# Attention, mixture of experts and MLP on one core: the first chunk's loads, splits and evacuations rearranged

## The chip, the cores and the metric

The kernel runs on one core of a Trainium2 chip. The metric is the device time of one execution in microseconds (us), the median of three runs. Before the change these were 749.26, 752.66 and 753.28 us, median 752.66.

## What is computed

Three stages follow each other, over two batches of 576 tokens.

```python
# attention: batch 2, heads 8, sequence 576, head size 64
scores = q @ k.T / 8
cum = cumsum(log(clip(f, 1e-4, 1)))                 # per head, along the sequence
scores = where(causal, -1e9, scores + cum[:, None] - cum[None, :])
attn = softmax(scores) @ v
x = attn as (1152 tokens, 512)
# mixture of 4 experts, 512 -> 1024 -> 512
p = domain_probs / (domain_probs.sum(-1) + 1e-9)
out = sum over e of p[:, e] * (relu(x @ w1[e]) @ w2[e])
# MLP, 512 -> 2048 -> 512
h = out @ w_in
y = (h * sigmoid(1.702 * h)) @ w_out
```

## The kernel before

**Tiles and stages.** The 1152 tokens form four chunks: chunk 0 is batch 0, tokens 0 to 255; chunk 1 the other 320 tokens of that batch; chunks 2 and 3 the same of batch 1. Attention of a chunk goes in units. A unit of chunk 0 is one head (eight units); a unit of the others is a head pair and 128 queries. Each unit passes scores on TensorE (L367), the row maximum on VectorE (L394), the exponential on ScalarE (L408), the sum's reciprocal on VectorE (L414, L415), the normalisation on GpSimd (`e`, L417), transposes on TensorE (`t`, L435), copies of them to SBUF (`ph`, L53), and per head pair the product with the values (`x`, L462). From it come `xh` (rounded, ScalarE L53) and `xl` (the rest, VectorE L471). Every expert or MLP product is made as three matmuls (hi by hi, hi by lo, lo by hi), so each weight tile is split into `whi` and `wlo` (`split_w`: `whi` on ScalarE L53 or GpSimd L50, `wlo` on VectorE L159).

**Order.** Attention and expert visits are interleaved by a pulling loop: while the experts' products of one chunk run, units of the next are pulled. While chunk 0 is pulled, the first expert half is multiplied head pair by head pair (`emit_first`, L551); the next visits use L530 and L574. Within an engine the instructions stand in the order that the tile scheduler chose by its own simulation of the timeline; each engine then works that list off in order.

**Loads.** Nearly all DMAs are issued by SP on one hardware queue: `fr` (gates), `kd`, `qd`, `vd` of head groups 0 to 3 and 4 to 7 of chunk 0, `wst` (two expert weight tiles, 512 KB, two buffers that come free when both `wlo` are made), `kq` and `vd` of a later head pair, and per head pair `cb` (two, 256 KB) and `cbs` (288 KB). The last two are the cumulated gates broadcast over partitions, from a copy `cumd` in DRAM; `cbs` has the two heads' rows on 64 partitions each (L332). `prep_cum` loads them three units ahead (LEAD) and GpSimd adds a triangular mask to them (L326, L329 for `cb`, L335 for `cbs`). `dpT` and `dpb` are the experts' probabilities, written to DRAM and read back broadcast.

**Chunk 0's mask term.** The key tile `kd` holds 64 rows of keys; row 64 is the cumulated gate, brought by a DMA from `cum` (L300); the query tile holds a constant in that row (L294). Rows 65 to 127 are zeroed by memsets (L292, L293), and the product runs over 128 rows.

Of the kernel before, what the change touches and what calls it, by code (L numbers as in the profile page):

```python
# [32 lines left out]
def attn_moe_mlp(ctx: ExitStack, tc: tile.TileContext, qk0, qk1, qk2, v0, vp, fg, dp, wa_moe, wb_moe, wa_mlp, wb_mlp, outT):  # L33
# [15 lines left out]
    def round_pool(out, in_):  # L49
        nc.gpsimd.tensor_scalar(out=out, in0=in_, scalar1=1.0, scalar2=1.0, op0=ALU.mult, op1=ALU.mult)  # L50

# [96 lines left out]
    def split_w(kind, v_, g):  # L148
        raw = raw_w.pop((kind, v_, g))
        p = wa_p if kind == "a" else wb_p  # L150
        hi = p.tile([128, 4, 128], F32R, tag="hi", name="whi")
        lo = p.tile([128, 4, 128], F32R, tag="lo", name="wlo")
        hf = hi.rearrange("p a c -> p (a c)")
        lf = lo.rearrange("p a c -> p (a c)")
        (round_pool if late or v_ <= 2 and g == 3 else round_act)(hf, raw)
        (wa if kind == "a" else wb)[v_, g] = (hi, lo)

        def rest():
            nc.vector.tensor_sub(lf, raw, f(hf))  # L159
            if visits[v_][0] < NMOE:  # L160
                if g % 2:
                    load_pair()
            else:
                w_split_n[0] += 1

        lo_due.append(rest)
# [118 lines left out]
    def load_plain(h0):  # L285
# [4 lines left out]
        for i, t in enumerate((kd, qd)):  # L290
            nc.sync.dma_start(out=t[0:64], in_=qk0[h0 // G, i].rearrange("d (g s) -> d g s", g=G))
        nc.gpsimd.memset(kd[64:128], 0.0)  # L292
        nc.gpsimd.memset(qd[64:128], 0.0)  # L293
        nc.gpsimd.memset(qd[64:65], 1.0 / NEG)  # L294
        groups[h0] = (qd, kd, vd)

    def load_plain_rest(h0):
        G, wk = 4, SA
        qd, kd, vd = groups[h0]
        nc.sync.dma_start(out=kd[64:65], in_=cum[h0:h0 + G, :wk])  # L300
        nc.sync.dma_start(out=vd, in_=v0[h0 // G].rearrange("p (t g d) -> p t g d", t=2, g=G))
        for g in range(G):
            heads[0, h0 + g] = dict(vd=vd[:, :, g, :], qd=qd[:, g], kd=kd[:, g])

# [115 lines left out]
    def emit_tr(c, u):  # L420
# [7 lines left out]
        for k, (q0, off, w, _) in enumerate(todo):  # L428
# [3 lines left out]
            for k0, k1 in [(0, min(nk, 4))] + [(4, 5)] * (nk > 4):  # L432
# [4 lines left out]
                for j, h in enumerate(hs if w == S else hs[k:k + 1] if len(hs) > 1 else hs):  # L437
                    r = 64 if w == S else 128
                    ph = ph_of[c, h]
                    ph = ph[:, 3:4, 0:64] if k0 else ph[:, 0:k1, o:o + r]  # L440
                    round_act(ph, cols[:, :, j * r:(j + 1) * r])

# [169 lines left out]
    nc.sync.dma_start(out=fr, in_=fg)  # L612
    nc.vector.memset(ones, 1.0)
    load_plain(0)
    nc.gpsimd.memset(mask, 0.0)
    nc.gpsimd.affine_select(out=mask[:, 128:], in_=mask[:, 128:], pattern=[[-1, 128]],
# [6 lines left out]
    for a, z in ((0, SA), (SA, S)):  # L623
# [3 lines left out]
                                     initial=cum[:, a - 1:a] if a else 0.0, op0=ALU.mult, op1=ALU.add)  # L627
    load_plain_rest(0)
    load_plain(4)
    load_plain_rest(4)  # L630
    nc.vector.tensor_scalar(out=fr, in0=cum, scalar1=1.0 / NEG, scalar2=None, op0=ALU.mult)
    nc.sync.dma_start(out=cumd, in_=fr)
    for _ in range(2):
        load_pair()
    round_pool(tri, mask[:, 128:])
    make_probabilities()
    load_heads(passes[1], 0)
    nc.sync.dma_start(out=dpb0, in_=dpT[0:1, :S].to_broadcast([128, S]))
    nc.sync.dma_start(out=dpb1, in_=dpT[1:2, :DPB1].to_broadcast([128, DPB1]))

# [15 lines left out]
    while ready[0] < 0:  # L656
        pull()
        if pulled[0] in (7, 8, 9, 10):
            split_w("a", 0, pulled[0] - 7)
            split_rest()  # L660
        while x_made[0] > x_used[0] and pulled[0] > 10:
            emit_first(x_used[0])
            x_used[0] += 1
# [95 lines left out]
```

## Time and profile before

| what | value |
|---|---|
| median of the three runs | 752.66 us |
| the profiled execution's own time | 752.34 us |
| its span, first to last instruction | 750.4 us |
| mean granted TensorE clock | 0.991 of full speed |
| busy: TensorE, VectorE, GpSimd, ScalarE | 724.2, 470.1, 307.5, 220.9 us |
| bytes moved by DMA | 67.24 MB |

TensorE is busy nearly all the time, so a stretch is worth reading only where TensorE stands still or runs at the lower clock. A wait in the profile is written as the waiting engine and line, an arrow, and what came last of the things it waited for.

### The profile page before, as it was taken

Reading aid. Unit: us, or ns where it says so; the run is one execution under the profiler, and the core shown is the slowest. Engines: PE = TensorE matmul, PEld = TensorE weight load, DVE = VectorE, ACT = ScalarE, POOL = GpSimd, SP = SyncE. Lnnn points to the kernel's source line nnn. Section 1 sums busy time; section 2 is a strip of 40 time slices with the busy share of each in tenths; the row PEclk is TensorE's granted clock in tenths of the full one; section 3 lists DMA queues with packets and bytes.
Section 4 is the critical chain, followed back from the end, with each engine's and each line's share of the span. In section 5 each row is a group of like instructions: output and inputs, shape, how many; then the busy total and the mean of one; then the engine's idle time right before and its main releaser. Section 6 shows DMA issues by size and latency. Waiting matters only on the chain.

```text
span 750.4 us, 11873 instructions
## 1 busy us (share of the span) xinstructions
PE 724.2 (97%) x4424; PEld 669.9 (89%) x4424; DVE 470.1 (63%) x1015; ACT 220.9 (29%) x551; POOL 307.5 (41%) x402
## 2 busy tenths in 40 slices
PE   3989989999999999889999999999999999999998
PEld 2556769787799999889999999999999999999998
DVE  5546555666665999999964334343999865424422
ACT  4665544565632101101111111112323232222220
POOL 6546425343232324563363334443464445324420
PEclk9899989999999999999999999999999999999999
DMA  8656543421225544635321011100222200000012
GB/s 247 197 180 168 173 143 113 138 84 61 84 57 191 165 119 139 200 112 169 115 83 57 29 29 57 56 1 2 64 60 80 79 0 1 1 1 1 1 43 85
DMA packets 29497, 67.24 MB, mean 90 GB/s; under 512 B 3032, under 2 KB 4576, under 8 KB 29440
## 3 DMA queue, kind: packets, MB, share of 16 engines
q1 hardware_dynamic: 29440, 66.48, 28.7%
q8 instruction: 35, 0.57, 0.3%
q14 instruction: 22, 0.18, 0.1%
HBM read 64.05 MB, written 2.41 MB: 89 GB/s over the span
## 4 chain that ended last, share of the span: by engine, by line
PE 73%; DVE 16%; DMA 4%; issue 3%; POOL 2%; ACT 1%; SPq 0%; POOLq 0%; DVEq 0%; ACTq 0%
PE m L574 32%; PE m L530 29%; PE s L367 5%; DVE wlo L159 4%; PE x L462 3%; PE t L435 3%; DVE wf L214 2%; DVE cvd L220 2%; DVE wf L222 2%; DVE tmp L588 1%; DMA wst<-in_wb_moe_dram 1%; DMA wst<-in_wa_moe_dram 1%; DVE xl L594 1%; DVE cvt L206 1%; DVE cvt L217 1%
## 5 line engine op out<-in xcount | busy, mean ns | idle before, releaser
L590 POOL TENSOR_TENSOR acc<-acc,tmp 128x384 f32<-128x384 f32 (+3 forms) x112 | 104.5, 944 | 146.9 <-DVE tmp L588 128.6
L574 PE MATMUL m<-hh,wlo 128*128 128x384 f32 (+2 forms) x640 | 129.0, 322 | 3.8 <-DVE wlo L159 3.8
L574 PE MATMUL m<-hh,whi 128*128 128x384 f32 (+2 forms) x640 | 130.6, 324 | 0.3 <-DVE tmp L588 0.3
L574 PE MATMUL m<-hl,whi 128*128 128x384 f32 (+2 forms) x640 | 129.5, 322 | 0.0
L530 PE MATMUL m<-xh,whi 128*128 128x384 f32 (+2 forms) x624 | 127.4, 324 | 0.5 <-POOL whi L50 0.3
L556 ACT ACTIVATE hh<-m 128x384 fp32r<-128x384 f32 (+2 forms) x112 | 49.5, 444 | 263.4 <-PE m L530 252.1
L530 PE MATMUL m<-xh,wlo 128*128 128x384 f32 (+2 forms) x624 | 125.1, 321 | 1.3 <-DVE wlo L159 1.3
L530 PE MATMUL m<-xl,whi 128*128 128x384 f32 (+2 forms) x624 | 125.8, 321 | 0.0
L159 DVE TENSOR_TENSOR wlo<-wst,whi 128x512 fp32r<-128x512 f32 x112 | 97.7, 874 | 27.2 <-ACT whi L53 15.1
L574 PEld LDWEIGHTS m<-hh,wlo 128*128 128x128 f32 x640 | 106.4, 190 | 8.0 <-DVE wlo L159 5.2
L574 PEld LDWEIGHTS m<-hh,whi 128*128 128x128 f32 x640 | 106.8, 190 | 5.4 <-issue 4.0
L574 PEld LDWEIGHTS m<-hl,whi 128*128 128x128 f32 x640 | 106.8, 190 | 3.5 <-issue 3.4
L530 PEld LDWEIGHTS m<-xh,whi 128*128 128x128 f32 x624 | 103.5, 188 | 4.7 <-issue 1.8
L530 PEld LDWEIGHTS m<-xh,wlo 128*128 128x128 f32 x624 | 103.5, 188 | 3.0 <-DVE wlo L159 1.8
L530 PEld LDWEIGHTS m<-xl,whi 128*128 128x128 f32 x624 | 103.6, 188 | 2.3 <-issue 2.0
L565 POOL TENSOR_TENSOR hl<-tmp,hh 128x384 fp32r<-128x384 f32 x48 | 53.6, 1116 | 90.4 <-ACT hh L53 90.4
L557 DVE SCALAR_TENSOR_TENSOR hl<-m,hh 128x384 fp32r<-128x384 f32 (+2 forms) x112 | 55.2, 493 | 52.8 <-ACT hh L556 52.8
L50 POOL TENSOR_SCALAR whi<-wst 128x512 fp32r<-128x512 f32 x62 | 46.5, 757 | 71.9 <-issue 26.8
L588 DVE TENSOR_TENSOR tmp<-m,dpb 128x384 f32<-128x384 f32 (+2 forms) x80 | 40.8, 512 | 41.7 <-PE m L574 35.1
L417 POOL TENSOR_SCALAR e<-e,sm 128x128 f32<-128x128 f32 (+4 forms) x72 | 43.9, 621 | 35.2 <-DVE sm L415 22.2
L563 DVE TENSOR_TENSOR tmp<-m,sg 128x384 f32<-128x384 f32 x48 | 26.6, 555 | 45.9 <-ACT sg L562 45.8
L408 ACT ACTIVATE e<-e,mx 128x128 f32<-128x128 f32 (+4 forms) x72 | 41.9, 582 | 29.6 <-DVE mx L394 28.0
(74 smaller groups left out, 719.1 us busy)
## 6 DMA issues: line engine op xcount, KB each, us to landing
wst<-in_wa_moe_dram SPq DMA_DIRECT2D x28, 512.0 KB, 4.1
wst<-in_wb_moe_dram SPq DMA_DIRECT2D x28, 512.0 KB, 3.7
mst<-in_wa_mlp_dram SPq DMA_DIRECT2D x16, 512.0 KB, 3.9
mst<-in_wb_mlp_dram SPq DMA_DIRECT2D x16, 512.0 KB, 4.1
cb<-cumd SPq DMA_DIRECT2D x16, 256.0 KB, 5.7
vd<-in_vp_dram SPq DMA_DIRECT2D x8, 320.0 KB, 7.5
kq<-in_qk_dram SPq DMA_DIRECT2D x4, 608.0 KB, 6.5
cbs<-cumd SPq DMA_DIRECT2D x8, 288.0 KB
```

The source lines that it names most:

```text
L50: nc.gpsimd.tensor_scalar(out=out, in0=in_, scalar1=1.0, scalar2=1.0, op0=ALU.mult, op1=ALU.mult)
L159: nc.vector.tensor_sub(lf, raw, f(hf))
L367: nc.tensor.matmul(pt[:, :z - a], lhsT=l, rhs=r, start=True, stop=True)
L408: nc.scalar.activation(out=e[:, off:off + w], in_=e[:, off:off + w], func=AF.Exp, scale=-1.0, bias=mx, accum_out=sm[:, 0, k:k + 1])
L417: nc.gpsimd.tensor_scalar(out=e[:, off:off + w], in0=e[:, off:off + w], scalar1=sm[:, 0, i:i + 1], scalar2=1.0, op0=ALU.mult, op1=ALU.mult)
L530: nc.tensor.matmul(p[:, :n], lhsT=w[:, k, :], rhs=x[c][:, k, :], start=(j == 0 and k == 0), stop=(j == 2 and k == 3))
L556: nc.scalar.activation(out=hh[:, g, :n], in_=p[:, :n], func=AF.Relu)
L557: nc.vector.scalar_tensor_tensor(out=hl[:, g, :n], in0=p[:, :n], scalar=0.0, in1=f(hh[:, g, :n]), op0=ALU.max, op1=ALU.subtract)
L565: nc.gpsimd.tensor_sub(hl[:, g, :n], t[:, :n], f(hh[:, g, :n]))
L574: nc.tensor.matmul(p[:, :n], lhsT=w[:, k, :], rhs=x[:, k, :n], start=(j == 0 and k == 0), stop=(j == 2 and k == 3))
L588: nc.vector.tensor_mul(t[:, :n], p[:, :n], d)
L590: nc.gpsimd.tensor_add(a, a, t[:, z])
```

## The change

- Both head groups' `kd`, `qd`, `vd` are loaded first; the two `kd` gate rows follow behind all six, after the first 256 tokens are cumulated.
- Score products of chunk 0 run over 65 rows instead of 128, and the four large memsets go (`[:65]`).
- A dummy logarithm is issued before the gates land.
- The load order after `cumd` becomes: one `wst`, one `kq` and `vd`, the other `wst`. `make_probabilities` goes behind the sixth pulled unit and the broadcasts `dpb` behind the ninth.
- The first expert half's four `whi` are made on GpSimd instead of ScalarE, and are held, with their `wlo`, at their place in program order, behind the normalisations of the units pulled before them.
- The 256-column `ph` copies of chunk 0 go to VectorE.

```diff
     def round_pool(out, in_):
-        nc.gpsimd.tensor_scalar(...)
+        return nc.gpsimd.tensor_scalar(...)
 ...
-        (round_pool if late or v_ <= 2 and g == 3 else round_act)(hf, raw)
+        if v_ == 0 and kind == "a":
+
+            tc.keep_in_program_order(round_pool(hf, raw))
+        else:
+            (round_pool if late or v_ <= 2 and g == 3 else round_act)(hf, raw)
 ...
-            nc.vector.tensor_sub(lf, raw, f(hf))
+            sub = nc.vector.tensor_sub(lf, raw, f(hf))
+            if v_ == 0 and kind == "a":
+                tc.keep_in_program_order(sub)
 ...
-        nc.gpsimd.memset(kd[64:128], 0.0)
-        nc.gpsimd.memset(qd[64:128], 0.0)
+        nc.sync.dma_start(out=vd, in_=v0[h0 // G].rearrange("p (t g d) -> p t g d", t=2, g=G))
+
         nc.gpsimd.memset(qd[64:65], 1.0 / NEG)
 ...
         nc.sync.dma_start(out=kd[64:65], in_=cum[h0:h0 + G, :wk])
-        nc.sync.dma_start(out=vd, in_=v0[h0 // G].rearrange("p (t g d) -> p t g d", t=2, g=G))
         for g in range(G):
-            heads[0, h0 + g] = dict(vd=vd[:, :, g, :], qd=qd[:, g], kd=kd[:, g])
+            heads[0, h0 + g] = dict(vd=vd[:, :, g, :], qd=qd[:65, g], kd=kd[:65, g])
 ...
-                    round_act(ph, cols[:, :, j * r:(j + 1) * r])
+                    if plain(c) and k1 == 2:
+                        nc.vector.tensor_copy(ph, cols[:, :, j * r:(j + 1) * r])
+                    else:
+                        round_act(ph, cols[:, :, j * r:(j + 1) * r])
 ...
     nc.vector.memset(ones, 1.0)
+
+    nc.scalar.activation(out=cum[:, :1], in_=ones[:, :1], func=AF.Ln)
     load_plain(0)
+    load_plain(4)
 ...
-    load_plain_rest(0)
-    load_plain(4)
-    load_plain_rest(4)
+        if a == 0:
+            load_plain_rest(0)
+            load_plain_rest(4)
 ...
-    for _ in range(2):
-        load_pair()
+    load_pair()
+    load_heads(passes[1], 0)
+    load_pair()
     round_pool(tri, mask[:, 128:])
-    make_probabilities()
-    load_heads(passes[1], 0)
-    nc.sync.dma_start(out=dpb0, in_=dpT[0:1, :S].to_broadcast([128, S]))
-    nc.sync.dma_start(out=dpb1, in_=dpT[1:2, :DPB1].to_broadcast([128, DPB1]))
 ...
         pull()
+        if pulled[0] == 6:
+            make_probabilities()
         if pulled[0] in (7, 8, 9, 10):
             split_w("a", 0, pulled[0] - 7)
             split_rest()
+        if pulled[0] == 9:
+            nc.sync.dma_start(out=dpb0, in_=dpT[0:1, :S].to_broadcast([128, S]))
+            nc.sync.dma_start(out=dpb1, in_=dpT[1:2, :DPB1].to_broadcast([128, DPB1]))
```

Three places show how the lists of the engines move. Numbers behind a name tell buffers apart. The `e` tiles of chunk 0's units 1 to 8 are, before, `e_189`, `e_205`, `e_229`, `e_253`, `e_284`, `e_320`, `e_355`, `e_383`; in the change `e_173`, `e_189`, `e_213`, `e_237`, `e_268`, `e_304`, `e_350`, `e_378`.

**SP's queue, the second set of gate broadcasts.** Before, from the second head pair's loads on:

```order
L311 DMA kq_326<-in_qk1_dram 128x960
L313 DMA vd_328<-in_vp_dram 128x640
L142 DMA wst_393<-in_wb_moe_dram 128x2x512
L323 DMA cb_395<-cumd_110 128x512
L323 DMA cb_399<-cumd_110 128x512
L332 DMA cbs_403<-cumd_110 128x1x576
L311 DMA kq_442<-in_qk1_dram 128x960
L256 DMA dpT_113<-dpn_169 128x4x9
L313 DMA vd_444<-in_vp_dram 128x640
L142 DMA wst_478<-in_wb_moe_dram 128x2x512
```

The change:

```order
L316 DMA kq_310<-in_qk1_dram 128x960
L318 DMA vd_312<-in_vp_dram 128x640
L254 DMA dpraw_314<-in_dp_dram 128x36
L328 DMA cb_390<-cumd_110 128x512
L328 DMA cb_394<-cumd_110 128x512
L337 DMA cbs_398<-cumd_110 128x1x576
L316 DMA kq_437<-in_qk1_dram 128x960
L318 DMA vd_439<-in_vp_dram 128x640
L262 DMA dpT_113<-dpn_315 128x4x9
L672 DMA dpb0_76<-dpT_113 128x576
L673 DMA dpb1_77<-dpT_113 128x576
L142 DMA wst_388<-in_wb_moe_dram 128x2x512
```

The first second-layer weights (`wst` from `in_wb`) stood in front of the second `cb`, `cb`, `cbs`; now they stand behind them and behind the trip of `dpT` through DRAM.

**GpSimd, the adds to `cbs`.** Before, from unit 6 on, with the second `cbs` between units 7 and 8:

```order
L417 TENSOR_SCALAR e_320<-e_320,sm_321 128x128
L417 TENSOR_SCALAR e_320<-e_320,sm_321 128x256
L417 TENSOR_SCALAR e_355<-e_355,sm_356 128x128
L417 TENSOR_SCALAR e_355<-e_355,sm_356 128x256
L326 TENSOR_TENSOR cb_395<-cb_395,tri_123 128x128
L329 TENSOR_TENSOR cb_395<-cb_395,tri_123 128x128
L326 TENSOR_TENSOR cb_399<-cb_399,tri_123 128x128
L329 TENSOR_TENSOR cb_399<-cb_399,tri_123 128x128
L335 TENSOR_TENSOR cbs_403<-cbs_403,tri_123 64x64 x2
L417 TENSOR_SCALAR e_383<-e_383,sm_384 128x128
L417 TENSOR_SCALAR e_383<-e_383,sm_384 128x256
```

The change, the first `cbs` (between units 3 and 4), and then from unit 5 to the first weight split:

```order
L422 TENSOR_SCALAR e_213<-e_213,sm_214 128x128
L422 TENSOR_SCALAR e_213<-e_213,sm_214 128x256
L331 TENSOR_TENSOR cb_274<-cb_274,tri_123 128x128
L334 TENSOR_TENSOR cb_274<-cb_274,tri_123 128x128
L331 TENSOR_TENSOR cb_278<-cb_278,tri_123 128x128
L334 TENSOR_TENSOR cb_278<-cb_278,tri_123 128x128
L340 TENSOR_TENSOR cbs_282<-cbs_282,tri_123 64x64 x2
L422 TENSOR_SCALAR e_237<-e_237,sm_238 128x128
```

```order
L422 TENSOR_SCALAR e_268<-e_268,sm_269 128x128
L422 TENSOR_SCALAR e_268<-e_268,sm_269 128x256
L331 TENSOR_TENSOR cb_394<-cb_394,tri_123 128x128
L334 TENSOR_TENSOR cb_394<-cb_394,tri_123 128x128
L340 TENSOR_TENSOR cbs_398<-cbs_398,tri_123 64x64 x2
L261 TENSOR_TENSOR dpn_315<-dpraw_314,dps_316 128x36
L422 TENSOR_SCALAR e_304<-e_304,sm_305 128x128
L422 TENSOR_SCALAR e_304<-e_304,sm_305 128x256
L50 TENSOR_SCALAR whi_356<-wst_160 128x512
```

The adds to the first `cbs` moved from behind unit 4 to in front of it, those to the second from in front of unit 8 to in front of unit 6. All first `whi` stand behind them.

On TensorE, the transposes `t` of a unit wait for its `e`. The first product with expert weights stands, before, between the transposes of unit 3; in the change behind those of unit 6. Ahead of unit 6's transposes TensorE's list holds, in the change, the transposes of units 1 to 5, the scores of units 1 to 8 but for the last wide product, and the value products of two head pairs.

**GpSimd, some 85 us into the run.** Before, from the fifth `cbs` to the sixth:

```order
L335 TENSOR_TENSOR cbs_904<-cbs_904,tri_123 64x64 x2
L385 MEMSET e_1044 128x64
L417 TENSOR_SCALAR e_928<-e_928,sm_929 128x384 x2
L326 TENSOR_TENSOR cb_1167<-cb_1167,tri_123 128x384
L329 TENSOR_TENSOR cb_1167<-cb_1167,tri_123 128x128
L50 TENSOR_SCALAR whi_1226<-wst_1054 128x512
L417 TENSOR_SCALAR e_984<-e_984,sm_985 128x512 x2
L326 TENSOR_TENSOR cb_1171<-cb_1171,tri_123 128x384
L329 TENSOR_TENSOR cb_1171<-cb_1171,tri_123 128x128
L417 TENSOR_SCALAR e_1044<-e_1044,sm_1045 128x576
L335 TENSOR_TENSOR cbs_1175<-cbs_1175,tri_123 64x64 x2
```

The change:

```order
L340 TENSOR_TENSOR cbs_901<-cbs_901,tri_123 64x64 x2
L390 MEMSET e_1041 128x64
L50 TENSOR_SCALAR whi_1223<-wst_1051 128x512
L422 TENSOR_SCALAR e_925<-e_925,sm_926 128x384 x2
L331 TENSOR_TENSOR cb_1164<-cb_1164,tri_123 128x384
L334 TENSOR_TENSOR cb_1164<-cb_1164,tri_123 128x128
L422 TENSOR_SCALAR e_981<-e_981,sm_982 128x512 x2
L331 TENSOR_TENSOR cb_1168<-cb_1168,tri_123 128x384
L334 TENSOR_TENSOR cb_1168<-cb_1168,tri_123 128x128
L422 TENSOR_SCALAR e_1041<-e_1041,sm_1042 128x576
L340 TENSOR_TENSOR cbs_1172<-cbs_1172,tri_123 64x64 x2
```

The weight split `whi` stood behind a normalisation and the two adds of a `cb`; now it stands right behind the adds to `cbs`. In SP's list the next `wst`, which takes the buffer that this split frees, stands before and now a few issues ahead of the sixth `cbs` (before `wst`, `vd`, `kq`, `cbs`; now `wst`, `cb`, `vd`, `kq`, `cbs`).

## Rows read from the trace of the kernel before

**Rows 1.** The page, part 1: busy time, share of the span and instructions of each engine, the row of TensorE.
```profile
PE 724.2 (97%) x4424; PEld 669.9 (89%) x4424; DVE 470.1 (63%) x1015; ACT 220.9 (29%) x551; POOL 307.5 (41%) x402
```

**Rows 2.** The list of waits of TensorE (PE) in the first 60 us: engine and line that waited, what it waited for, us in total, times, longest.
```profile
PE s L367 <- DMA kd<-fr: 8.2, 1, 8.2
PE s L367 <- DVE mx L394: 3.5, 2, 2.6
PE m L551 <- ACT xh L53: 2.0, 1, 2.0
PE t L435 <- POOL e L417: 0.7, 2, 0.4
```

**Rows 3.** The same list for ScalarE (ACT) in the first 60 us, the two waits for expert weights.
```profile
ACT whi L53 <- DMA wst<-in_wb_moe_dram: 3.4, 1, 3.4
ACT whi L53 <- DMA wst<-in_wa_moe_dram: 3.1, 1, 3.1
```

**Rows 4.** The table of stretches: from:to and length in us, then busy us (and instructions) of PE, PEld, DVE, ACT and POOL, the granted TensorE clock (1.00 is 2.4 GHz, 0.50 is 1.2 GHz), the busy share of the DMA engines and GB/s.
```profile
5.31:8.19 2.88, 0.00 (x0) 0.03 (x1) 2.15 (x2) 0.97 (x1) 2.67 (x4) 1.00 0.82 196
8.19:10.77 2.58, 2.48 (x7) 1.93 (x8) 1.02 (x6) 0.94 (x4) 0.48 (x1) 1.00 0.74 239
8.19:13.05 4.86, 4.76 (x13) 3.54 (x14) 1.79 (x10) 1.48 (x6) 1.31 (x3) 1.00 0.88 290
13.05:16.47 3.42, 0.84 (x5) 0.44 (x3) 1.37 (x4) 2.04 (x6) 0.64 (x2) 1.00 0.93 348
16.47:23.30 6.83, 5.24 (x14) 2.42 (x15) 3.59 (x18) 3.56 (x14) 5.67 (x13) 0.50 1.00 307
23.30:35.10 11.80, 11.80 (x68) 7.54 (x67) 7.33 (x36) 8.80 (x31) 6.05 (x14) 1.00 0.65 178
38.50:40.54 2.04, 0.04 (x1) 0.00 (x0) 0.29 (x1) 0.95 (x3) 0.75 (x3) 1.00 1.03 279
105.20:112.00 6.80, 6.80 (x28) 5.72 (x28) 2.54 (x8) 1.66 (x5) 2.38 (x5) 0.50 0.06 22
```

**Rows 5.** The timeline of TensorE: start, us, engine and line, operation, shapes, count. One wide score product of chunk 0 (it is recorded as two matmuls), early and later.
```profile
12.22 1.03 PE L367 MATMUL s<-kd,qd 128*128 128x256 f32 x2
24.39 0.60 PE L367 MATMUL s<-kd,qd 128*128 128x256 f32 x2
```

**Rows 6.** The chain of waits between 20 and 60 us, in order of time: start, us, what, count. Pieces of TensorE alone: a wide and a narrow score product of chunk 0, two transposes, and the two parts of one pair's product with the values.
```profile
26.85 0.45 PE s L367 x2
25.68 0.22 PE s L367 x2
25.46 0.22 PE t L435 x2
41.99 0.58 PE x L462 x2
44.83 0.79 PE x L462 x5
```

**Rows 7.** The timeline of GpSimd (POOL) in the first 40 us: start, us, line, operation, and in brackets the idle time in front of it.
```profile
0.80 0.95 POOL L292 MEMSET kd<- 64x1024 f32 x1 [0.29 <-POOLq L747]
...
15.83 0.62 POOL L50 TENSOR_SCALAR whi<-wst 128x512 fp32r<-128x512 f32 x1 [3.47 <-DMA wst<-in_wa_moe_dram]
...
23.86 0.82 POOL L417 TENSOR_SCALAR e<-e,sm 128x128 f32<-128x128 f32 x2 [1.39 <-DVE sm L415]
24.74 0.74 POOL L335 TENSOR_TENSOR cbs<-cbs,tri 64x64 f32<-64x64 f32 x2
...
35.79 0.70 POOL L335 TENSOR_TENSOR cbs<-cbs,tri 64x64 f32<-64x64 f32 x2 [3.90 <-PE m L551]
36.59 1.95 POOL L417 TENSOR_SCALAR e<-e,sm 128x128 f32<-128x128 f32 x4
```

**Rows 8.** The timeline of the DMA-issuing engine (SP), same columns: three issues in a row.
```profile
17.01 0.38 SPq L142 DMA_DIRECT2D wst<-in_wb_moe_dram  x1
17.43 0.94 SPq L323 DMA_DIRECT2D cb<-cumd  x2
18.56 0.54 SPq L332 DMA_DIRECT2D cbs<-cumd  x1
```

**Rows 9.** The DMA issues of 17.4 to 18.4 us: tile, engine, count, KB of each, median us from issue to landing.
```profile
cb<-cumd SPq DMA_DIRECT2D x2, 256.0 KB, 11.1
```

**Rows 10.** The chain of waits from the start: the first expert weights, from issue (8.29) to landing, us.
```profile
8.29 6.12 DMA wst<-in_wa_moe_dram
```

**Rows 11.** The timeline of ScalarE: the table load in front of the first logarithm.
```profile
2.64 1.28 ACT L625 ACT_TABLE_LOAD   x1 [2.64 <-DMA fr<-in_fg_dram]
```

**Rows 12.** The timeline of GpSimd around the stop at 102 us.
```profile
84.86 1.05 POOL L335 TENSOR_TENSOR cbs<-cbs,tri 64x64 f32<-64x64 f32 x2 [8.51 <-DMA cbs<-cumd]
...
88.71 0.62 POOL L50 TENSOR_SCALAR whi<-wst 128x512 fp32r<-128x512 f32 x1
...
103.32 0.70 POOL L335 TENSOR_TENSOR cbs<-cbs,tri 64x64 f32<-64x64 f32 x2 [9.69 <-DMA cbs<-cumd]
```

**Rows 13.** The timeline of TensorE there.
```profile
104.54 0.68 PE L435 MATMUL t<-identr,e 128*128 128x128 f32 x2 [2.45 <-POOL e L417]
```

**Rows 14.** The timeline of SP there.
```profile
90.60 0.38 SPq L142 DMA_DIRECT2D wst<-in_wa_moe_dram  x1
...
92.06 0.52 SPq L332 DMA_DIRECT2D cbs<-cumd  x1
```

More of the change, by code (lines that the diff above doesn't have):

```diff
@@ L49, in round_pool @@
     def round_pool(out, in_):
-        nc.gpsimd.tensor_scalar(out=out, in0=in_, scalar1=1.0, scalar2=1.0, op0=ALU.mult, op1=ALU.mult)
+        return nc.gpsimd.tensor_scalar(out=out, in0=in_, scalar1=1.0, scalar2=1.0, op0=ALU.mult, op1=ALU.mult)
     def round_act(out, in_):
```

## Prediction, before the change was run

> **What bounds the kernel now.** I read the page first: TensorE is busy 724.2 us, 97% of the span [rows 1], so the time is TensorE's work plus the few places where it stands still or runs slowly. The list of its waits and the table of stretches then show where these are early on. It stands 8.2 us until the first gate row is in `kd`, 3.5 us in two waits for row maxima and 2.0 us for `xh` [rows 2]. Behind the 2.6 us wait for a maximum lies a weight: ScalarE stood 3.1 us in front of a `whi` whose `wst` had not landed, and all that was queued behind it waited too; behind the 2.0 us wait a second one of 3.4 us [rows 3]. After the first of these stops come 6.83 us at the granted clock 0.50, the 1.2 GHz level [rows 4]. A further stop lies at 102 us: TensorE waits 2.45 us for a normalisation [rows 13] that stands on GpSimd behind the adds to a `cbs`, and these waited 9.69 us for their load [rows 12]; 6.80 us at 1.2 GHz follow [rows 4].
>
> **The start.** The four memsets of about 1 us each [rows 7] and the table load of 1.28 us [rows 11] end before the first gate row lands, so taking them off that path is worth nothing: TensorE's wait ends with a DMA. Of the products over 65 rows I expect nothing either: they keep their 128 or 256 columns, and the trace has no 65-row product; eight units of 0.22 + 0.45 us [rows 6] are 5.4 us, of which a tenth either way, 0.5 us, bounds it. The gate rows now stand behind two more loads, 512 KB in all, which at the 196 and 239 GB/s of the stretches around 8 us [rows 4] are 2.2 to 2.7 us, at the 348 GB/s soon after 1.5. I take the first product at 10 us instead of 8.2. That alone does not enter the sum, since a later wait ends last.
>
> **The adds to `cbs` on GpSimd.** Nothing of the weights holds the heads any more, so the 2.6 and 2.0 us stops go. What takes their place is named in the order: GpSimd now stands at the first `cbs` before unit 4's normalisation and at the second before unit 6's. Before, the first add began at 24.74 without a wait, the second at 35.79 after 3.90 us of idle time [rows 7]. The list names a TensorE product as the releaser of the second, but the add waits for a DMA: the `cb` issued at 17.43 and 17.90 took 11.1 us, so they were in at 28.5 and 29.0, and `cbs`, issued behind them, needs the 6.7 us up to 35.7 [rows 8, 9].
>
> When will it land in the change? In front of it goes one `wst` from `in_wb`. A `wst` costs 1.4 us of the queue (the first two were issued together; one was in at 14.41, the other was taken up at 15.83) [rows 7, 10]: 34.3. The DMA engines stood idle 18% and 26% of the two stretches around the gate rows [rows 4], 1.2 us together, which may now be filled: 33.1. I take 33.5. Why the load is slow decides how low it can go. If it was held up by the transfers beside it, it gets faster with fewer of them. The Trainium skill, DMA: Bandwidth & Descriptors, in "Why a DMA increments its semaphore by 16 and not by 1", says that a DMA runs on the largest number of engines up to 16 that divides the outermost dimension of both sides, which is 2 for this load of two heads; at the 27.2 GB/s per port that follow from its "Where 436 GB/s comes from" (435.2 over 16), half of 288 KB takes an estimated 5.4 us however quiet the rest is. By that quieter surroundings would gain 1.3 us at most, and the sum would be 1.3 us lower; the row's 6.7 us agrees with it as a floor, and no row shows the load alone. From rows alone I use 6.7 us. The upper bound of the landing is 34.3. For the lower one the two stretches around the gate rows run at 348 GB/s instead of 196 and 239 [rows 4]: 2.88 + 2.58 us become 1.6 + 1.8, 2.1 less, 32.2.
>
> From the adds to the first transpose behind them the stop at 102 us took 1.2 us (103.32 to 104.54) [rows 12, 13]. Here one small operation, `dpn`, stands between; I add 0.4, half of a pair of normalisations [rows 7]. So unit 6's transposes start at 35.1 (33.8 to 35.9).
>
> **How far behind that is.** By then the change has done, on TensorE, eight narrow and seven wide scores (0.22 and 0.45 us), the transposes of five units (three at 0.11 each) and the value products of two pairs (0.58 and 0.79) [rows 6]: 1.8 + 3.2 + 1.7 + 2.7 = 9.3 us of work at full clock. Before, up to 35.10 it was busy 4.76, 0.84, 5.24 and 11.80 us [rows 4]. The first and third count half (the third at clock 0.50; in the first a wide product took 1.03 us against 0.60 later [rows 5]), the second I put at 0.6: 17.4 us of work. So the change is 8.1 us of work behind, of which the 2.0 us stop at 38.5 to 40.54 gives back 2.0: **6.1 us later** (4.8 to 6.9 at the two ends).
>
> TensorE stands idle for over half of the time from 10 to 35 us in the change. Before, stops of 2.58 and 2.45 us were each followed by some 6.8 us at 1.2 GHz [rows 4]; if such a stretch covers the work that follows unit 6, it costs up to 3.4 us. I take half, 1.7. The `in_wb` weights now stand behind `dpT`'s trip through DRAM. From `dpn` at 34.5, one landing at the 6.1 us of [rows 10] and 2.8 us for two broadcasts (two `cb` sizes) and one `wst` give 43.5; ScalarE makes two `whi` in front of `xh` of the last pair, which TensorE reaches 11 us after 35.1. Covered by some 2 us; if not, 0 to 1 us more.
>
> VectorE takes over eight copies of 256 columns, about 0.4 us each by ScalarE's rate; it is busy 7.33 of 11.80 us there, ScalarE 8.80 [rows 4], so these stay beside other work. The first `whi` on GpSimd (0.62 each [rows 7]) stand behind the waits just priced and in front of units 7 to 9; TensorE has 8 us of overdue products then, which hide them.
>
> **What may come back at 102 us.** The sixth `cbs` was issued at 92.06, 1.5 us behind a `wst` at 90.60 [rows 14], which needed the buffer that the `whi` at 88.71 frees. The order now puts this `whi` right behind the adds that began at 84.86 and took 1.05 [rows 12], so near 86.1: up to 2.6 us earlier. The stop is 2.45 us. If that much reaches the `cbs`, the stop goes and the slow stretch behind it, 2.45 + 6.80/2 = **5.9 us**. The schedule beyond that point issues the same work, so I carry nothing else.
>
> **Sum.** 752.34 (the profiled execution, 0.32 below the median of its three runs) + 6.1 + 1.7 - 5.9 = 754.2.
>
> **Rivals.**
> 1. *Slower: the stop at 102 us stays.* If the `wst` is issued earlier but the `cbs` behind it is held by something else (its buffer, the queue's backlog, which was 11 us deep there by rows 12 and 14: 92.06 to 103.3), the early loss stands alone: 752.3 + 6.1 + 1.7 = 760.1. It decides where less than about 1 us of the 2.6 reaches the load, since a stop of 2.0 us was not followed by the low clock at 38.5 [rows 4] and one of 2.45 was. For it: that load spent over 11 us between issue and landing. Chance 0.28.
> 2. *Faster: GpSimd does not hold the heads.* If the second `cbs` lands by about 27, units run at their own pace, and what goes is 2.6 + 0.9 of the maximum waits, 0.7 for normalisations, 2.0 for `xh` [rows 2] and the 2.6 us lost to the low clock after 16.47, less 1.8 at the start: 7 us, less 2 to 5 for units paced by the row maxima, and 0 to 5.9 at 102 us: about 747. Against it: 6.7 us for one such load, two of them in the queue. Chance 0.17.
> 3. *Nothing much on either side:* the early loss is 1 to 3 us, for instance since the loads fill the queue better than I think, and 102 us stays: 753 to 756. Chance 0.10.
>
> **How the numbers follow.** Chance of the forecast (early loss, most of it regained at 102 us) 0.45. About 0.5%, 3.8 us, is what a measurement of this kernel can tell from no change: 748.6 to 756.1 against the profiled time. The forecast's own range, 4.8 to 6.9, clock 0 to 3.4, less 3.5 to 5.9, is 751.2 to 759.1; about a quarter of it is above 756.1. So slower 0.11 + 0.28 = 0.39, faster rival 2 and a little of 3: 0.18, same 0.43. The range 747.0 to 761.0 leaves out the better half of rival 2 and the worse third of rival 1.
>
> **What would show it.** In the profile after: first product near 10 us; in TensorE's waits none for row maxima over 1 us, but transposes waiting for a normalisation, twice, for several us, around 24 and 35 us; GpSimd's waits naming `cbs` there; the first expert product after 35 us; the granted clock at 0.50 between 20 and 40 us; no stop behind the sixth `cbs`. Wrong if expert products run before 32 us, if GpSimd's adds to the first two `cbs` begin without a wait, or if the loss at 102 us is there as before.

## The result and the profile after

The change takes 761.14 us (median of four runs, 758.79 to 764.22); the kernel before, run beside it, 751.10. The ratio is 1.0122, with an interval of 1.0096 to 1.0149: slower by some 10 us where the forecast was 2 us. The median lies 0.1 us beyond the upper end of the range given, 761.0. It is near rival 1's 760.1, but not by rival 1's mechanism: the stop at 102 us is gone, as forecast. The profiled execution took 759.3 us, with a span of 757.6 against 750.4. TensorE's row of the page, and the longest of its waits over the whole span:

```profile
PE 731.4 (97%) x4424; PEld 674.7 (89%) x4424; DVE 471.1 (62%) x1023; ACT 217.1 (29%) x541; POOL 306.4 (40%) x401
```

```profile
PE s L372 <- DMA cumd<-fr: 10.0, 1, 10.0
PE m L538 <- ACT whi L53: 4.3, 1, 4.3
PE t L440 <- POOL e L422: 3.0, 3, 2.1
PE m L582 <- DVE wlo L163: 2.9, 4, 1.1
```

TensorE is busy 7.2 us more than in [rows 1] for the same work, which is all of the difference of the spans. Standing still has only moved: 10.0, 4.3 and 3.0 us now, against 8.2, 3.5 and 2.0 [rows 2] and the 2.45 us at 102 us [rows 13]. So the loss is TensorE working slowly. Its timeline (start, us, and in brackets the idle time in front) shows where:

```profile
14.04 1.08 PE L372 MATMUL s<-kd,qd 65*128 65x256 f32 x2
...
19.25 1.06 PE L372 MATMUL s<-kd,qd 65*128 65x256 f32 x2
...
23.57 0.48 PE L440 MATMUL t<-identr,e 128*128 128x128 f32 x1 [0.75 <-POOL e L422]
...
32.81 0.47 PE L440 MATMUL t<-identr,e 128*128 128x128 f32 x1 [2.07 <-POOL e L422]
33.08 1.06 PE L372 MATMUL s<-kd,qd 65*128 65x256 f32 x2
...
35.54 0.58 PE L559 MATMUL m<-xh,whi 128*128 128x256 f32 x1
```

Every wide score of chunk 0 takes 1.06 us or more, and the first expert product starts at 35.54. In the kernel before, it fell from 1.03 to 0.60 [rows 5], by 24.4 us, and the first expert product started at 24.64:

```profile
24.64 0.47 PE L551 MATMUL m<-xh,whi 128*128 128x256 f32 x1
```

1.06 is the pace of the 1.2 GHz level (a run below has it at a granted clock of 0.51), 0.60 that of 2.4 GHz. The table of stretches (busy us and count of PE, PEld, DVE, ACT, POOL; granted clock; DMA share; GB/s) does not say so:

```profile
10.00:20.00 10.00, 9.90 (x29) 6.83 (x29) 5.48 (x28) 4.99 (x20) 4.15 (x10) 1.00 0.98 351
20.00:30.00 10.00, 9.25 (x31) 5.19 (x31) 3.50 (x18) 3.38 (x14) 4.78 (x14) 1.00 0.35 124
30.00:40.00 10.00, 7.93 (x26) 4.04 (x24) 4.78 (x21) 2.77 (x11) 5.14 (x12) 1.00 0.24 75
...
60.00:70.00 10.00, 9.35 (x38) 5.96 (x40) 6.34 (x16) 5.85 (x17) 5.23 (x8) 0.66 0.48 133
...
100.00:130.00 30.00, 29.66 (x219) 23.73 (x215) 20.25 (x62) 16.52 (x49) 15.41 (x24) 1.00 0.50 153
130.00:760.00 630.00, 618.99 (x3816) 596.79 (x3815) 400.81 (x783) 154.09 (x362) 247.76 (x289) 0.99 0.23 72
```

The clock column reads 1.00 from 10 to 40 us while products take 1.06. This text goes by the durations there; that the clock itself stood at the 1.2 GHz level is inferred from them. The Trainium skill, TensorE: Matmul & The Clock Gate, in "Seeing it yourself", says that recorded clock events on this chip have been seen to be unreliable; this trace agrees. The last row dates the loss: 3816 products are left after 130 us, where the same table of the kernel before has 3761:

```profile
100.00:130.00 30.00, 27.53 (x191) 23.84 (x190) 14.01 (x32) 11.53 (x27) 13.02 (x21) 0.89 0.37 113
130.00:760.00 630.00, 611.12 (x3761) 589.07 (x3760) 397.40 (x775) 150.94 (x356) 242.60 (x283) 1.00 0.23 70
```

At 618.99 / 3816 = 0.162 us each these 55 are 8.9 us, so all of the loss has arisen before 130 us.

GpSimd stood where the prediction put it (its timeline, then ScalarE's, then one piece of the chain of waits):

```profile
22.34 0.70 POOL L340 TENSOR_TENSOR cbs<-cbs,tri 64x64 f32<-64x64 f32 x2 [3.06 <-DMA cbs<-cumd]
...
31.34 0.70 POOL L340 TENSOR_TENSOR cbs<-cbs,tri 64x64 f32<-64x64 f32 x2 [3.22 <-DVE mx L399]
```

```profile
59.97 1.15 ACT L53 ACTIVATE whi<-wst 128x512 fp32r<-128x512 f32 x2 [4.71 <-DMA wst<-in_wa_moe_dram]
```

```profile
48.63 11.31 DMA wst<-in_wa_moe_dram
```

For the second add the trace names a row maximum on VectorE as what ended the wait. That it waited for its load is inferred: the load was still running until about then (below), and the wait is gone in the run that loads `cbs` in two parts.

The last two rows are a stop that was not forecast. The first `wst` of the next visit (from `in_wa`, the third behind the heads' loads) is issued at 48.63, right behind the third `cbs` (48.02), and lands 11.31 us later. ScalarE's `whi` waits for it, TensorE stands 4.28 us until 60.65, and then works at a low clock (0.66 in the 60 to 70 us row).

Why a `cbs` is slow can be read off the load rate while the second one is alone in the queue (stretch, clock, DMA share, GB/s):

```profile
26.00:31.00 5.00, 1.00 0.13 52
```

A share of 0.13 is two of 16 engines, and 288 KB (294,912 bytes) at 52 GB/s are 5.7 us. The prediction cited the Trainium skill, DMA: Bandwidth & Descriptors, "Why a DMA increments its semaphore by 16 and not by 1", for two engines and an estimate of 5.4 us; the trace agrees with the two engines, and with the estimate to 0.3 us.

### The profile page after: what moved, and what is told of

The parts are those of the page before. It is cut to its first block, busy times and chain, and to the rows that moved or that the text cites. A ratio compares the mean times of both kernels' runs of the same rounds, so it can differ in the third digit from the quotient of the medians.

```text
span 757.6 us, 11863 instructions
## 1 busy us (share of the span) xinstructions
PE 731.4 (97%) x4424; PEld 674.7 (89%) x4424; DVE 471.1 (62%) x1023; ACT 217.1 (29%) x541; POOL 306.4 (40%) x401
## 4 chain that ended last, share of the span: by engine, by line
PE 69%; DVE 19%; DMA 6%; issue 3%; POOL 2%; ACT 0%; SPq 0%; POOLq 0%; DVEq 0%; ACTq 0%
PE m L582 30%; PE m L538 28%; PE s L372 5%; DVE wlo L163 4%; PE x L470 3%; DMA wst<-in_wa_moe_dram 3%; PE t L440 3%; DVE cvd L226 2%; DVE wf L228 2%; DVE wf L220 2%; DVE tmp L596 1%; DMA mst<-in_wa_mlp_dram 1%; DVE xl L602 1%; DVE cvt L212 1%; DVE cvt L223 1%
## 5 line engine op out<-in xcount | busy, mean ns | idle before, releaser
L582 PE MATMUL m<-hh,whi 128*128 128x384 f32 (+2 forms) x640 | 128.7, 321 | 0.2 <-DVE tmp L596 0.2
L538 PE MATMUL m<-xh,wlo 128*128 128x384 f32 (+2 forms) x624 | 127.1, 324 | 0.6 <-DVE wlo L163 0.6
L50 POOL TENSOR_SCALAR whi<-wst 128x512 fp32r<-128x512 f32 x65 | 49.9, 775 | 71.0 <-issue 27.0
```

Source lines behind the costliest of these rows:

```text
L50: return nc.gpsimd.tensor_scalar(out=out, in0=in_, scalar1=1.0, scalar2=1.0, op0=ALU.mult, op1=ALU.mult)
L538: nc.tensor.matmul(p[:, :n], lhsT=w[:, k, :], rhs=x[c][:, k, :], start=(j == 0 and k == 0), stop=(j == 2 and k == 3))
L582: nc.tensor.matmul(p[:, :n], lhsT=w[:, k, :], rhs=x[:, k, :n], start=(j == 0 and k == 0), stop=(j == 2 and k == 3))
```

## Experiments

In most runs below each engine's list was held in the order of the kernel named, apart from the move that is described. It was not held in the two runs that first load `cbs` in two parts. The change kept its lists there all the same. In the kernel before three things moved forward: SP issues `dpT` at 19.73 instead of 25.78 us, and the `dpb` loads ahead of a `wst`, and GpSimd adds to half of the first `cbs` one head earlier. "Products over 128 rows" means the old form with its memsets. The kernel before, run again beside them, had medians of 752.17, 752.25 and 751.11 us. Theory A: products over 65 rows hold TensorE at the 1.2 GHz pace. Its rival: the late `cbs` and weights set the time, and the pace only decides whether their waits show.

### First set: rows, and the load of cbs, each in both kernels

**The change with 128 rows.**

```diff
+        nc.gpsimd.memset(kd[64:128], 0.0)
+        nc.gpsimd.memset(qd[64:128], 0.0)
...
-            heads[0, h0 + g] = dict(vd=vd[:, :, g, :], qd=qd[:65, g], kd=kd[:65, g])
+            heads[0, h0 + g] = dict(vd=vd[:, :, g, :], qd=qd[:, g], kd=kd[:, g])
```

> The change with its score products of chunk 0 over all 128 rows again (the four memsets are back), every engine's list held in the change's own order. Theory A (the products over 65 rows are what keeps TensorE at its 1.2 GHz pace from 10 to 41 us): a wide score product falls from 1.06 to 0.60 us some 5 us after the first one, as it did before the change, the first expert product comes before 35.5, and the time falls by 4 to 9 us, to 752 to 757. Theory B (it is the thin work, since no expert products lie between the heads, and the waits for cbs): wide products stay at 1.06 until about 40 us and the time stays within 2 us of the change's 761.

Measured: 765.24 us, ratio 1.016 (1.0124 to 1.0196): no gain, and 4 us above the change, which neither theory had. TensorE's timeline:

```profile
18.38 0.60 PE L383 MATMUL s<-kd,qd 128*128 128x256 f32 x2
...
25.14 0.48 PE L451 MATMUL t<-identr,e 128*128 128x128 f32 x1 [4.78 <-POOL e L433]
25.41 1.06 PE L383 MATMUL s<-kd,qd 128*128 128x256 f32 x2
...
34.39 0.47 PE L451 MATMUL t<-identr,e 128*128 128x128 f32 x1 [2.89 <-POOL e L433]
```

The pace does rise (0.60 at 18.38), as theory A wants. But TensorE then waits 4.78 and 2.89 us for GpSimd behind the two `cbs`, and after the first stop the wide score takes 1.06 again. With the fast pace the heads run into the late loads; the slow pace had covered part of this (0.75 and 2.07 us of waiting there).

**The kernel before with 65 rows** (the same edit the other way round).

> The kernel before with only the products of chunk 0 over 65 rows and without the four memsets, every engine's list held in the order of before. Theory A: wide products stay at 1.06 us past 13 us and past 23.3 us, where before they had gone to 0.60, and the time rises by 2 to 8 us. Theory B: no change, within 1.5 us of before, since the expert products lie between the heads as before and the memsets were covered.

Measured: 749.84 us, ratio 0.9976 (0.9958 to 0.9994). The pace stayed slow longer, as expected: a wide score took 1.06 at 24.36 and 0.60 at 28.47, with expert products over 128 rows from 24.86 on between them. The time did not rise; it lies 2.3 us lower, a little more than theory B allowed. So 65 rows alone cost nothing in that order; theory A's pace came, its price did not.

**The change, and then the kernel before, with each cbs in two loads** of 64 partitions:

```diff
-        nc.sync.dma_start(out=st["cbs"], in_=cumd[r:r + 2, :].unsqueeze(1).to_broadcast([2, 64, S]))
+        for g in range(2):
+            nc.sync.dma_start(out=st["cbs"][64 * g:64 * g + 64],
+                              in_=cumd[r + g:r + g + 1, :].to_broadcast([64, S]))
```

> The change with each cbs loaded as two loads of 64 partitions, one per head, in place of one load with the two heads outermost; TensorE's, VectorE's and ScalarE's lists of the first chunk stay. If the load's slowness is its two engines: each cbs lands in about 1 us instead of 5 to 7, GpSimd waits no more than 1 us for one, the first expert weights of the second visit land 5 us sooner and the 4.3 us stop at 56 us goes. Theory A then leaves TensorE at the slow pace in the first chunk, so the time falls by 6 to 10 us, to 751 to 755. Theory B expects the slow pace to end by 25 us as well, and 745 to 750.

> The kernel before with each cbs loaded as two loads of 64 partitions; TensorE's and VectorE's lists are those of before. The 2.45 us stop at 102 us and the 6.8 us at 1.2 GHz behind it go, 5.9 us, and the loads behind each cbs land sooner, so the stop for xh at 38.5 (2.0) shrinks: 743 to 747. If the slowness of cbs is the queue's load and not its two engines: no change, 750 to 753.

Measured: the change 748.08 us, ratio 0.9938 (0.9904 to 0.9973); the kernel before 744.94, ratio 0.9892 (0.9861 to 0.9923). GpSimd's adds to the first two `cbs` in the change, and two of TensorE's wide scores there:

```profile
19.19 0.70 POOL L341 TENSOR_TENSOR cbs<-cbs,tri 64x64 f32<-64x64 f32 x2
...
24.70 0.71 POOL L341 TENSOR_TENSOR cbs<-cbs,tri 64x64 f32<-64x64 f32 x2
```

```profile
22.79 1.06 PE L373 MATMUL s<-kd,qd 65*128 65x256 f32 x2
...
25.08 0.59 PE L373 MATMUL s<-kd,qd 65*128 65x256 f32 x2
```

The change's time lies in theory B's range and below theory A's, and the pace rose by 25 us as theory B said. No bracket stands behind either add: the waits of 3.06 and 3.22 us are gone, and so are the stops at 23, 33 and 60 us. In the change that is worth 13 us, in the kernel before 7 (there together with the few moves in its lists named above). The ten runs of the changed kernel lie at 742.1 and 742.4, at 747.8 to 748.5 (five) and at 752.0 to 752.3 (three); the profile is of one of the two quickest. In it the pace rose by 25.08, with scores over 65 rows, before the first expert product (28.36): the transposes and value products between the scores run over 128 rows.

### Second set: which of the two waits, and 128 rows with the quick load

**GpSimd's adds behind the heads.** In GpSimd's list of the change, the adds to the first `cbs` (L350), those for the second pair, and the probabilities (`dps`) go behind the normalisations of all eight heads (L432); VectorE's part of `dps` goes along.

```diff
-L350 TENSOR_TENSOR cbs<-cbs,tri 64x64 x2
 L432 TENSOR_SCALAR e<-e,sm 128x128
 L432 TENSOR_SCALAR e<-e,sm 128x256
 ...
+L350 TENSOR_TENSOR cbs<-cbs,tri 64x64 x2
```

> The change with one thing moved on GpSimd: the adds to both cbs, the probabilities and the second pair's adds to cb stand behind the normalisations of all eight heads; VectorE's one operation on the probabilities moves with them. All other lists are the change's. Theory G (GpSimd's waits for cbs in front of units 4 and 6 cost the first chunk its time, by standing still and by the 1.2 GHz pace that follows): transposes of unit 4 start by 21 us instead of 23.6, those of unit 6 by 27 instead of 32.8, expert products by 30 instead of 35.5, and the time falls by 4 to 8 us, to 753 to 757; the stop at 56 us stays or grows, since the second-layer weights are late for another reason. Rival (TensorE was busy at 1.2 GHz anyway, so the waits were covered): under 2 us.

Measured: 761.94 us, ratio 1.0125 (1.0096 to 1.0154), no different from the change. The heads' waits for GpSimd went and the first expert product came at 31.89 instead of 35.54. But TensorE then stood 2.46 us for a row maximum, and the later stop grew (TensorE's timeline, then SP's):

```profile
38.87 1.60 PE L382 MATMUL s<-kq 64*128 64x512 f32 x2 [2.46 <-DVE mx L409]
...
63.47 1.22 PE L548 MATMUL m<-xh,whi 128*128 128x256 f32 x4 [5.11 <-ACT whi L63]
```

```profile
39.46 0.38 SPq L272 DMA_DIRECT2D dpT<-dpn  x1
```

The delay comes from the edit itself. With the probabilities behind the heads, `dpT` is issued at 39.46 instead of 32.43; the `in_wb` weights behind it in SP's list follow at 44.16 instead of 40.42, and the late `wst` at 52.39 instead of 48.63. So this run does not show that the waits at units 4 and 6 are free: what was won in front of the expert products (3.65 us) was lost again behind them.

**The late weights ahead of the third cbs.** In SP's list:

```diff
-L347 DMA cbs<-cumd 128x1x576
 L152 DMA wst<-in_wa_moe_dram 128x2x512
+L347 DMA cbs<-cumd 128x1x576
 L152 DMA wst<-in_wa_moe_dram 128x2x512
```

> The change with two neighbours in SP's list exchanged: the first wst of the second visit goes ahead of the third cbs instead of behind it. Theory (the 4.3 us stop at 56.4 and the slow stretch behind it come from that wst landing behind a cbs of 6 us): the wst lands near 53 instead of 59.9, the stop goes, the time falls by 6 to 8 us, to 753 to 755. Rival (the cbs is needed as soon): the stop moves to the transposes behind the third cbs and the time stays within 2 us of the change's.

Measured: 755.66 us, ratio 1.0034 (1.0009 to 1.0059), 5.5 us below the change, where 6 to 8 were expected. No wait for `whi` on ScalarE is left in TensorE's list:

```profile
PE s L382 <- DMA cumd<-fr: 10.1, 1, 10.1
PE t L450 <- POOL e L432: 3.3, 3, 2.1
```

So the stop at 60 us, 4.28 us and the low clock behind it, is worth more than half of the loss of 10.0 us: 5.5 us by the medians, 6.6 by the ratios (1.0122 less 1.0034).

**The change with cbs in two loads and 128 rows** (both edits above).

> The change with each cbs as two loads, and with the products of chunk 0 over 128 rows again, lists as in the run with two loads. Theory A (65-row products keep TensorE at 1.2 GHz longer when nothing else stops it): wide products reach 0.60 us by 17 us instead of 25, and the time falls by 2 to 4 us against the run with two loads, to 744 to 746. Rival (the pace depends on when a run happens to start, not on rows): within 1.5 us of that run's 748 and the same spread of 742 to 752.

Measured: 743.19 us (four runs, 743.02 to 744.01), ratio 0.9878 (0.9851 to 0.9906). That is 4.9 us below the two loads with 65 rows, and the three groups of times became one. Two of the ten runs with 65 rows were as quick as these, so the 4.9 us are a difference of medians and not of every execution. The wide score is at 0.60 from early on, and what waits are left for GpSimd are short:

```profile
18.14 0.60 PE L384 MATMUL s<-kd,qd 128*128 128x256 f32 x2
...
21.11 0.33 PE L452 MATMUL t<-identr,e 128*128 128x128 f32 x1 [0.98 <-POOL e L434]
...
24.39 0.33 PE L452 MATMUL t<-identr,e 128*128 128x128 f32 x1 [1.30 <-POOL e L434]
```

### The pace by itself

Two probes put 48 products of 256 columns of a constant tile, without a gap, ahead of everything in the change. They differ only in the rows of these products; chunk 0's own scores have 65 rows in both.

```diff
+    for _ in range(48):
+        nc.tensor.matmul(warm[:, :256], lhsT=wtile[:65, :128], rhs=wtile[:65, :256], start=True, stop=True)
```

> The change with 48 products of 256 columns over 65 rows of a constant tile ahead of everything on TensorE, whose result is not used, to read when TensorE's pace changes under gapless work. Theory A: they stay at 1.2 GHz pace (0.85 us for one product, recorded as two) for more than 12 us, perhaps to the end. Rival: full pace (0.43) after 4 to 7 us as with 128 rows before the change.

> The control of the probe of 65 rows: the same 48 products of 256 columns of a constant tile without a gap ahead of everything, but over 128 rows; all the rest of the kernel is the change, with its 65-row products. If the 65 rows are what keeps TensorE at the 1.2 GHz pace: 0.86 us a product-pair half at first, then 0.43 after some 4 to 7 us of products, so that the 96 halves take 22 to 26 us in place of 41.3, and the time is 778 (between 774 and 781) in place of 795.7. If instead any product in the first microseconds of a kernel, or of a constant tile, runs at that pace: 41 us again, and 795.

Measured: 795.73 us with 65 rows, 768.56 with 128 (one run each). The probe with 65 rows and a wide score behind it:

```profile
1.85 41.33 PE L641 MATMUL m<-wtile 65*128 65x256 f32 x96 [1.85 <-DVE wtile L637]
42.96 3.66 PE L384 MATMUL s<-kd,qd 65*128 65x128 f32 x10
...
46.86 1.09 PE L384 MATMUL s<-kd,qd 65*128 65x256 f32 x2
```

The one with 128 rows:

```profile
1.84 23.98 PE L641 MATMUL m<-wtile 128*128 128x256 f32 x96 [1.84 <-DVE wtile L637]
25.67 2.26 PE L384 MATMUL s<-kd,qd 65*128 65x128 f32 x10
...
28.79 0.60 PE L384 MATMUL s<-kd,qd 65*128 65x256 f32 x2
```

Forty-one microseconds of work without a gap over 65 rows never left the slow pace: 0.43 us for each of 96. Over 128 rows the same 96 took 24.0 us. And chunk 0's wide scores over 65 rows, which follow, run at 0.60 us once the pace is up: such products do not slow TensorE here, and 41 us of them alone do not raise its pace. The heads begin 17.3 us earlier in the second probe, the time is 27.2 us less, so the slow pace goes with 9.9 us where the first two `cbs` have long landed (in neither probe do the adds to them wait). From the first head to the first expert product it is 6.0 us:

```profile
64.97 0.58 PE L571 MATMUL m<-xh,whi 128*128 128x256 f32 x1
```

```profile
41.68 0.38 PE L571 MATMUL m<-xh,whi 128*128 128x256 f32 x1
```

That is 22.0 us from 42.96 with 65 rows, and 16.0 from 25.67 with 128. Where the other 3.9 us arise was not pursued; both probes still have the late stop for `whi`, of 4.95 and 4.88 us. It is one run of each, and runs of the change spread by 5 us. The expected time, 778, counted the probe's own part alone; it was 9 us too high. (Its 0.86 us is that of a whole product at the slow pace; a recorded half takes 0.43, as the 41.33 us for 96 show.)

### Third set: combinations, and the first product

**The change with 128 rows and the late weights first** (two edits from above).

> The change with products over 128 rows (with the memsets) and the first-layer weights that follow the heads loaded ahead of the third cbs. Pace theory (65-row products cost the change some 5 us whatever else waits): 755.7 less 5, some 750.5. Rival (the two slow loads of cbs set the time of the first 40 us, the pace only decides whether their waits show): 754 to 757, with TensorE waiting 4 to 5 us at 25 and 2 to 3 us at 34 as in the change over 128 rows alone, and no wait for whi at 60.

Measured: 758.68 us, ratio 1.009 (1.0059 to 1.0121), where the same with 65 rows had 1.0034: not 5 us less, but 3 more. Against theory A, for its rival: with `cbs` in one load, TensorE waits 4.65 and 2.89 us for GpSimd, and the early pace is worth nothing. The time lies 1.7 us above the rival's range too.

```profile
24.41 0.48 PE L451 MATMUL t<-identr,e 128*128 128x128 f32 x1 [4.65 <-POOL e L433]
...
33.57 0.48 PE L451 MATMUL t<-identr,e 128*128 128x128 f32 x1 [2.89 <-POOL e L433]
```

**The best version with the first gate row ahead** of the second group's `qd` and `vd`:

```diff
 L307 DMA kd<-in_qk_dram 64x1024
+L317 DMA kd<-fr 1x4x256
 L307 DMA qd<-in_qk_dram 64x1024
+L317 DMA kd<-fr 1x4x256
 L308 DMA vd<-in_v_dram 128x512
-L317 DMA kd<-fr 1x4x256 x2
```

> The change with cbs in two loads and products over 128 rows, and the row of gates of the first four heads issued ahead of the second group's qd and vd, as in the kernel before. If the first product waits only for that row: it starts at 8.2 to 9.0 in place of 10.7, and as nothing else waits there the time falls by 1.5 to 2.5, to 741 to 742. Rival: the later qd and vd of the second group, or cb, take its place, and the time stays at 743.

Measured: 744.36 us, ratio 0.9907 (0.988 to 0.9935): no gain over 743.19, although the first product starts at 8.26 instead of 10.66. TensorE's timeline:

```profile
15.76 0.60 PE L384 MATMUL s<-kd,qd 128*128 128x256 f32 x2
...
21.69 0.48 PE L452 MATMUL t<-identr,e 128*128 128x128 f32 x1 [3.95 <-POOL e L434]
21.96 1.06 PE L384 MATMUL s<-kd,qd 128*128 128x256 f32 x2
```

The heads only reach the adds to `cb` and `cbs` earlier, wait 3.95 us there, and go on at half the pace: the granted clock of 20 to 30 us is 0.51. The early start was spent on a stop.

**The kernel before with cbs in two loads and 65 rows.**

> The kernel before with cbs in two loads (744.94) and products over 65 rows without the memsets. There no slow load of cbs hides the pace. Pace theory: TensorE stays at the 1.2 GHz pace until some 28 us in place of some 24, and the time is 2 to 4 us more, 747 to 749. Rival (the pace of the first 30 us is hidden by waits in any case): 744 to 746.

Measured: 745.77 us, ratio 0.9922 (0.9898 to 0.9946), 0.8 us above 744.94 with 128 rows, within the intervals. In that order the expert products over 128 rows begin at 24.29, and the wide score is at 0.60 by 27.63 (26.69 with 128 rows). So in this order 65 rows cost nothing that these runs can tell.

## Why the prediction was wrong in size

The runs make a square; each entry is the median in us:

| | cbs in one load | cbs in two loads |
|---|---|---|
| before, 128 rows | 752.17 | 744.94 |
| before, 65 rows | 749.84 | 745.77 |
| change, 65 rows | 761.14 | 748.08 |
| change, 128 rows | 765.24 | 743.19 |

With one load the change costs 11.3 us (65 rows) or 13.1 (128). With two loads it costs 2.3 us with 65 rows, and nothing with 128 (743.19 against 744.94); in both cases the intervals of the two ratios overlap. So the rearrangement itself costs nothing that these runs can tell. It loses time because it puts what the heads and weights need behind loads of `cbs` that run on two engines: this the column with two loads shows.

By the prediction's own steps:

- **The start.** Right: the first product at 10.00. That it "does not enter the sum" holds too: 2.4 us earlier bought nothing in the run with the gate row ahead. The stops for row maxima and for `xh` went, as forecast.
- **Adds to `cbs` in front of units 4 and 6.** The place was right, the time too late: the second add came at 31.34, so its load was in before the range of 32.2 to 34.3, and unit 6's transposes started at 32.81 instead of 35.1. About 1.0 of the 2.2 us is the load itself, 5.7 us alone where 6.7 was used; the rest is the queue in front of it. The signs came in part: the first expert product after 35 us, as said, but the waits of the transposes were 0.75 and 2.07 us, not several, and the low pace from 20 to 40 us stands in the durations and not in the granted clock (1.00).
- **Products over 65 rows: "nothing", at most 0.5 us.** The reasoning failed. It asked how long one such product takes, and a 65-row product does take no longer at either pace. It did not ask what raises the pace. The scores over 128 rows went, and the first expert products over 128 rows moved from 24.64 to 35.54. The wide scores of all heads then ran at the 1.2 GHz pace, so TensorE was busy there (9.90, 9.25 and 7.93 us of each 10), not "idle for over half of the time". Its price shows only where the first two `cbs` are not late: 4.9 us between medians with `cbs` in two loads, 9.9 in the probes. In the change as it stands 128 rows win nothing back (765.24 against 761.14), since the waits take the place of the slow pace; so this is not what the sum missed.
- **"In_wb weights: covered by some 2 us; if not, 0 to 1 us more."** This is the term that failed in the sum, by being stopped one load too soon. The `in_wb` weights themselves were covered. But the two `wst` buffers are taken until 48 us, and the next `wst`, behind the third `cbs`, took 11.31 us to land. The stop at 60 us and its slow stretch are 5.5 us by the medians of the run with the weights first, 6.6 by its ratio.
- **102 us.** Right: no stop of over 1 us there, and TensorE is busy 29.66 us from 100 to 130 us, against 27.53 before.
- **The sum.** 4035 products are left after 100 us, against 3952 before: 83 more, of which 28 are made up for by 130 us, 4.5 us at 0.162 each, where 5.9 was forecast. The span grew by 7.2 us, so the early loss is 7.2 + 4.5 = 11.7, against 7.8 (6.1 and 1.7). The same table tells when it arose, before the change and after:

```profile
0.00:50.00 50.00, 35.54 (x165) 21.88 (x166) 26.57 (x101) 26.85 (x80) 27.92 (x60) 0.93 0.72 215
50.00:100.00 50.00, 50.00 (x313) 35.08 (x314) 32.12 (x107) 31.56 (x90) 23.99 (x39) 1.00 0.55 175
```

```profile
0.00:50.00 50.00, 37.08 (x135) 22.25 (x136) 24.57 (x97) 20.78 (x63) 23.53 (x56) 1.00 0.58 183
50.00:100.00 50.00, 45.72 (x262) 31.93 (x262) 25.46 (x83) 25.70 (x68) 19.67 (x34) 0.93 0.53 164
```

By 50 us 30 products are missing, and 51 more by 100 us. Shared out by these counts, some 4 us of the 11.7 belong to the heads and some 7 to what follows, the stop at 60 us above all. This is an estimate, since products differ in length. By it the heads lost less than the 7.8 us forecast, and the stop that was not forecast is more than all that the sum missed. (The prediction's 17.4 us of work before adds up to 17.3; that moves nothing.)

Rival 1 had about the right size for the wrong reason, since its stop did go, and it is rival 1's price that stretched the range to 761.0: that the result came out so near its end is luck. The forecast's own range ended at 759.1. Rival 2 rested on a second `cbs` in by 27; it was late by 4 us.

What stays open: the changes of order were not tried together (adds behind the heads and weights first), and the run with the adds behind the heads delayed the weights as well; so whether the adds' place costs anything once the late weights are out of the way is not known. Nor is why the change with `cbs` in two loads has three groups of times; that 128 rows make them one speaks for a pace that rises early in some executions and late in others, but only one of the quick ones was profiled.

## What to carry to other kernels

When a stop is taken away, ask what its engine will reach earlier, and whether that has landed: here three ways of being earlier (128 rows, adds out of the way, an earlier first product) bought nothing in the forms tried, while taking the slow load off its two engines bought 7 us in the kernel before, 13 in the change and 22 in the change with 128 rows. The load's form is read from the DMA share while it is alone: 0.13 of 16 engines is two. And compare durations of one product form along the span before trusting that a busy TensorE is a fast one.

The Trainium skill, DMA: Bandwidth & Descriptors, "Rules for kernel authors", advises a multiple of 16 as the outermost dimension; the runs with two loads of 64 partitions agree, 13.1 and 7.2 us.

## What was not expected of the hardware

- Products over 65 rows, 41.3 us of them without a gap, did not bring TensorE to its fast pace; over 128 rows the same ones did within 24.0 us. At the fast pace, scores over 65 rows, with transposes and value products over 128 rows between them, kept it: 0.60 us a wide score through the heads of the second probe. In the profiled run of the change with `cbs` in two loads the same mixture rose to it by 25 us.
- The records gave a granted clock of 1.00 for 10 to 40 us of the change while a wide score took 1.06 us. After stops of 4.78, 3.95 and 4.28 us they did show it low (0.68 of 20 to 30 us in the change with 128 rows, 0.51 and 0.66 in the others).
- TensorE's stops of 0.98 and 1.30 us in the best version were followed by wide scores of 0.60 us; those of 3.95 and 4.78 us by 1.06.
